# A fused two-layer forward and backward kernel: gradient-job operands stored feature-major and turned when they are loaded, normalised rows turned by SyncE

## The chip, the cores and the metric

The kernel runs on one core of one Trainium2 chip. The metric is the device time of one execution in microseconds (us). The engines are named as in the profile: PE is TensorE (PEld its weight loads), DVE VectorE, ACT ScalarE, POOL GpSimd, SP SyncE. SP and POOL also issue DMAs; in the profile's DMA tables SP's queue is q1 and POOL's is q0. All large data are bf16.

## The reference

Four residual layers are run forward, `x = x + A(norm(x))`, `x = x + B(norm(x))`, and both once more with the same weights, and then the gradients of all inputs are taken against `grad_out`. There are 2048 rows of 448 features; the hidden width of B is 1792.

```python
def _A_ref(q, k, v, shift_k, ssm_k, ssm_D):
    ...                                   # k_shift: causal 4-tap filter of k
    kv = k_shift * v
    ...                                   # y: long convolution of kv with ssm_k, by FFT
    y = y + kv * ssm_D[None, None, :]
    return q * y
def _B_ref(x, w1, w2):
    h = jnp.einsum("bsd,df->bsf", x, w1)
    h = _silu(h)
    return jnp.einsum("bsf,fd->bsd", h, w2)
x = A_q
x = x + _A_ref(_layernorm(x, axis=-1), A_k, A_v, A_shift_k, A_ssm_k, A_ssm_D)
x = x + _B_ref(_layernorm(x, axis=-1), B_w1, B_w2)
x = x + _A_ref(_layernorm(x, axis=-1), A_k, A_v, A_shift_k, A_ssm_k, A_ssm_D)
x = x + _B_ref(_layernorm(x, axis=-1), B_w1, B_w2)
```

The outputs are x and the gradients of q, k, v, shift_k, ssm_k, ssm_D, w1 and w2. `y` does not depend on x, so both A layers share it.

## The kernel before, in words

The work has three stages.

The **head** (class `Head`, up to about 95 us) computes `y` by matrix products that form an FFT.

The **flow** (class `Flow`, about 95 to 480 us) handles 16 tiles of 128 rows. For each tile `j`, `Flow.tile` lists: normalise, gate with y, normalise (n1); turn n1 so that features lie on partitions (`turn`); the up product with w1 (`up`, lines 645 to 655); silu and its slope (`silu`); the down product with w2 (`down`, L689); the same again for layer 2 with n3; then the backward pass, whose up product with w2T is in `grad_up` and whose down product with w1T is in `back`. It yields, in feature-major form (128 features on partitions, 14 feature blocks, 128 rows): the activations of the two B layers (`a1`, `a2`, tile `aT`) and the two hidden gradients (`gh1`, `gh2`, tile `ghT`). Three operands per tile are turned by PE in `turn`: n1, n3 and G2 (four transposes at L627 into PSUM, then one copy to SBUF by ACT or DVE at L92 or L94). The incoming gradient `g` is turned by two DMA transposes on SP (L757, L758).

The **tail** (class `Tail`, about 455 us to the end) has the backward FFT and the weight gradients. The weight gradient of w2 needs `a` with rows on partitions, and that of w1 needs `gh` with rows on partitions. So in the flow `store_turned` turns each of the four tensors of a tile with one DMA transpose from SBUF to SBUF (tile `turned`, L679) and stores the result row-major in DRAM (`A_d`, `GH_d`, L680). The tail's `jobs` then takes 7 jobs of 256 features per weight. A job loads two pieces of 1 MB (16 row tiles of 128 rows by 256 features, tile `jb`, L1072), one for each layer: group 0 is layer 2 (`A_d[1]` against `grad_out`, or `GH_d[1]` against n3), group 1 is layer 1 (`A_d[0]` against G2, or `GH_d[0]` against n1). It runs 64 products (L1124), 16 for each of two 128-feature halves and each group. In this text load (p, g) is that of job p and group g. `jb` has three buffers; every second job's load of group 0 for w1 goes to a fourth, in the place of `Minv`. The rows of n1 and n3 come back from DRAM as `nmov` (L1055). The last tile's activations are not read from DRAM by the first two w2 jobs: they take them from the `turned` tile itself (`lastA`).

The order is not written by hand. Each operation is listed with its costs per engine, its dependencies and a priority, and a planner (`Sched.plan`) simulates the engines: whenever an engine is free it takes, among the operations that are ready and have buffers, the one with the lowest priority number. A DMA's time in this simulation comes from `RATE` (bytes per us) and one shared time `dma_free`. The operations are emitted in the planned order; at run time each engine and each queue executes its list strictly in order and waits on semaphores. A tile's priorities are spaced by `T_ = 20`; layer 2 starts at `c = b + T_`, the first layer's gradient at `d = c + T_`. `BUFS` gives the number of buffers of each tag. `k.load` chains the job loads (`behind`), so that they are issued in the order in which they are listed.

Of the kernel before, what the change touches and what calls it, by code (L numbers as in the profile page):

```python
# [13 lines left out]
BF16 = mybir.dt.bfloat16  # L14
# [6 lines left out]
P = 128  # L21
S = 2048
D = 448
F = 1792
J = 16
NT = 16
DC = 112
ND = 4
# [104 lines left out]
class Sched:  # L133
# [4 lines left out]
    STEP = 20  # L138
    RATE = {"plain": 300e3, "turn": 160e3}

# [98 lines left out]
    def plan(self):  # L239
# [3 lines left out]
        events = [0.0]  # L243
        dma_free = 0.0
        for o in self.all:
# [26 lines left out]
        t = 0.0  # L272
        total = sum(1 for o in self.all if o.cost)
        while len(order) < total:
            moved = True
            while moved:
                moved = False
                for e, q in queue.items():
# [10 lines left out]
                    o = best  # L289
# [38 lines left out]
            t = events[0]  # L328
# [250 lines left out]

T_ = 20.0  # L580
EARLY = 2
ROWS = (0, 128, 256, 320)
TURNED = ((1, 0), (1, 1), (3, 0))


class Flow:
# [31 lines left out]

    def turn(self, src, pr, tag, after=()):
        nc, k, s = self.nc, self.k, self.s  # L620
        pt = s.vb("ps", "d", [P, ND, P], BF16, "ps_t")
        nT = self.small(tag, (P, ND, P))
        nT.name = "nT"

        def mm(e):
            for b, lo in enumerate(ROWS):
                nc.tensor.transpose(pt[:, b, :], src[:, lo:lo + P], k.ident[:])  # L627
# [47 lines left out]

    def store_turned(self, src, dst, j, pr):
        nc, s = self.nc, self.s
        an = self.small("turned", (P, NF, P))
        self.k.last_turn_out = s.op({"SP": 2.2}, lambda e: nc.sync.dma_start_transpose(out=an[:], in_=src[:].rearrange("p a s -> p (a s)")), r=[src], w=[an], prio=pr, dma=("turn", 458e3))  # L679
        s.op({"SP": 0.4}, lambda e: nc.sync.dma_start(out=dst[:, j, :], in_=an[:].rearrange("p a f -> p (a f)")), r=[an], w=[self.k.st_[(id(dst), j)]], prio=pr + 3, dma=("plain", 458e3))  # L680
        return an

# [41 lines left out]
    def tile(self, j):  # L724
        nc, s, k = self.nc, self.s, self.k
        b = T_ * j
# [11 lines left out]
        s.op({"POOL": 0.6}, lambda e: nc.gpsimd.dma_start(out=_pm(k.N_d[0][:])[:, j, :], in_=n1[:]), r=[n1], w=[k.st_[("n", 0, j)]], prio=b + 10, dma=("plain", 115e3))  # L738
        a1, s1 = self.silu(self.turn(n1, b - 3, "nT1"), 0, b, (j, 0) in TURNED)
        self.store_turned(a1, k.A_d[0], j, b + 4)  # L740
        po = self.down(a1, k.w2, "ps_o", b + 8.6)
# [10 lines left out]
        k.lastA_op = k.last_turn_out  # L752
        g = self.small("g")
# [6 lines left out]
        k.lastG = self.last_up  # L760
        self.store_turned(gh2, k.GH_d[1], j, c + 15)
        po2 = self.down(a2, k.w2, "ps_o", c + 14.2)
# [35 lines left out]
class Tail:  # L798
# [242 lines left out]
    def jobs(self, which, pr):  # L1041
        nc, s, k = self.nc, self.s, self.k
        if which == "w2":
            k.load = []
            gm = s.vb("res", "W1", [P, NT, D], BF16, "gmov")
            gs = [gm.sub() for _ in range(4)]
            gl = [lambda i=i: s.op({"SP": 0.4}, lambda e: nc.sync.dma_start(out=gm[:, 4 * i:4 * i + 4, :], in_=_pm(k.grad_out[0])[:, 4 * i:4 * i + 4, :]), w=[gs[i]], prio=pr - 30, dma=("plain", 458e3), behind=[k.lastA_op]) for i in range(4)]
            groups = [(k.A_d[1], [gs[t // 4] for t in range(NT)], lambda t: gm[:, t, :]), (k.A_d[0], k.G2v, lambda t: k.G2[:, t, :])]
        else:
            nm = [s.vb("PF", ("A1", "B1v")[i], [P, NT, D], BF16, "nmov") for i in range(2)]  # L1050
            nh = [[v.sub() for _ in range(2)] for v in nm]
            for i in (1, 0):
                for h in range(2):
                    hs = slice(8 * h, 8 * h + 8)
                    s.op({"SP": 0.4}, lambda e, i=i, hs=hs: nc.sync.dma_start(out=nm[i][:, hs, :], in_=_pm(k.N_d[i][:])[:, hs, :]),  # L1055
                         r=[k.st_[("n", i, j)] for j in range(8 * h, 8 * h + 8)], w=[nh[i][h]], after=self.done[i], prio=pr - 30 if i else pr + 0.5, dma=("plain", 917e3))
            groups = [(k.GH_d[1], [nh[1][t // 8] for t in range(NT)], lambda t: nm[1][:, t, :]), (k.GH_d[0], [nh[0][t // 8] for t in range(NT)], lambda t: nm[0][:, t, :])]
        out7 = k.outs[7].rearrange("(c p) f -> p c f", p=DC)
# [8 lines left out]
        def bring(p, gi, lo, hi, at=None):  # L1067
            b, part, spare = fetch(p, gi, which == "w1" and (2 * p + gi) % 4 == 0)
            src = groups[gi][0]
            v = b.sub()  # L1070
            part[lo:hi] = [v] * (hi - lo)
            k.load = [s.op({"SP": 0.4}, lambda e: nc.sync.dma_start(out=b[:, lo:hi, :], in_=src[:, lo:hi, 256 * p:256 * p + 256]),  # L1072
                 r=[k.st_[(id(src), j)] for j in range(lo, hi)], w=[v], prio=pr + 12.5 * p + gi if at is None else at, dma=("plain", 65e3 * (hi - lo)), behind=k.load, after=self.done[0] if spare else ())]

# [80 lines left out]
def kernel(  # L1155
# [22 lines left out]
    nc = tc.nc  # L1178
    k = K()
# [32 lines left out]
    with tc.manual_schedule(engines={E.PE, E.Activation, E.DVE, E.Pool, E.SP}):  # L1212
# [5 lines left out]
    "res": dict(W1=1, W2=1, G2=1, Y=1),  # L1218
    "J": dict(jb=3, oo=2),
    "S": dict(KK=1, A1K=1, A1v=1, pq=3, skb=1, skc=1),  # L1220
    "E": dict(x0=3, w2T=1, st=2, mv=6, ve=6, n0=5, t1=1, x1=3, n1=5, nT1=1),
    "PM": dict(w2Tr=1, w1T=1, nT3=1, nTg=2, nTG=1, s1=4, T=4, turned=3, x2=1, n2=3, x3=3, n3=3, s2=2, g=3, ghp=2, ob=2,
               u=3, cp=6, junk=1, cc=6, tt=1, G3=2, gy2=3, G1=1, gy=1, gq=2),
# [104 lines left out]
```

## Time and profile before

| | us |
|---|---|
| median of 3 runs | 720.97 (719.65 to 722.09) |
| profiled execution | 722.94 |
| its span, first to last instruction | 721.2 |
| PE busy in it | 695.1 (96%) |
| DVE busy | 516.7 (72%) |
| ACT busy | 419.8 (58%) |
| L627 transposes of n (128) and G (64), PE busy | 12.5 and 6.2 |

| DMA | count, KB each | us to landing |
|---|---|---|
| jb<-GH_d, SP | 14, 1024 | median 7.2 |
| jb<-A_d, SP | 12, 1024 | median 7.4 |
| turned<-aT and turned<-ghT, SP, transposes | 32 each | median 5.5 |
| A_d<-turned, SP | 32, 448 | median 3.9 |
| GH_d<-turned, SP | 32, 448 | median 4.2 |

(The profile's table counts by tensor name, so the 32 of each pair are the two layers' 16 tiles.) A row of the profile's timeline reads: start in us, length in us, engine, line, operation, output tile <- input tiles, shapes, count; the part in brackets is idle time of that engine before it and what ended it. PE's matrix products are pipelined: a product's length contains its drain, and the next one starts before it ends, so the pace is read from start to start. In the rows of 20 us the numbers are the busy time of PE, PEld, DVE, ACT and POOL with instruction counts, then the granted clock, the DMA engines' mean busy share and GB/s. The share of DMA can exceed 1, because a packet's time counts in the stretch in which it starts.

### The profile page before, as it was taken

What the parts mean: (1) busy time and instruction counts of PE and PEld (TensorE: products, weight loads), DVE (VectorE), ACT (ScalarE), POOL (GpSimd) and SP (SyncE); (2) the same over time, 40 slices, a digit from 0 to 9 for tenths busy, and PEclk for the clock granted to TensorE, in tenths of its full rate; (3) what the DMA queues carried; (4) which work ended last, traced back from release to release, by engine and by line L of the source; (5) the groups of instructions that cost most, each with busy time, mean ns of one, the idle gap of its engine ahead of it and who ended that gap; (6) DMA issues with size and microseconds to landing.
All of it is one profiled execution on the core that took longest, in us unless ns stands there. A gap on an engine that the chain in (4) does not pass through costs nothing. (4 is left out here: it accounts for less than half of the span.)

```text
span 721.2 us, 18320 instructions
## 1 busy us (share of the span) xinstructions
PE 695.1 (96%) x7664; PEld 484.8 (67%) x7664; DVE 516.7 (72%) x1215; ACT 419.8 (58%) x518; POOL 158.9 (22%) x266
## 2 busy tenths in 40 slices
PE   6999879999999999999999999999999999999997
PEld 5887657777777777777777776655576766555553
DVE  4989775669988889888988867671479857959100
ACT  4899876586667765776667755521676555111311
POOL 1244153112321233222321211003123203100000
PEclk9999998999999999999999999999999999999999
DMA  9989988899889898888878798979759949996751
GB/s 323 275 236 291 344 143 179 183 217 210 190 187 190 213 202 179 190 208 226 167 181 188 205 213 200 305 217 280 214 181 370 319 139 329 354 292 191 193 130 27
DMA packets 230720, 160.08 MB, mean 222 GB/s; under 512 B 145326, under 2 KB 207966, under 8 KB 230252
## 3 DMA queue, kind: packets, MB, share of 16 engines
q1 hardware_dynamic: 216862, 117.85, 66.6%
q0 software_dynamic: 13008, 40.24, 17.3%
q8 instruction: 60, 0.98, 0.6%
q10 hardware_dynamic: 766, 0.80, 0.3%
q14 instruction: 24, 0.20, 0.1%
HBM read 65.36 MB, written 54.60 MB: 166 GB/s over the span
## 5 line engine op out<-in xcount | busy, mean ns | idle before, releaser
L1124 PEld LDWEIGHTS <-jb 128*128 128x128 bf16 x892 | 85.7, 98 | 77.8 <-DMA jb<-GH_d 1.2
L645 PE MATMUL ps_h<-nT,w1sb 128*128 128x128 bf16 x1344 | 88.0, 222 | 5.7 <-DVE nT L94 4.9
L689 PE MATMUL ps_n<-w1T,ghT 128*128 128x448 bf16 x448 | 90.0, 352 | 1.4 <-ACT u L788 0.9
L689 PE MATMUL ps_o<-w2sb,aT 128*128 128x448 bf16 x448 | 90.1, 353 | 0.0
L645 PEld LDWEIGHTS <-w1sb 128*128 128x128 bf16 x1344 | 79.4, 99 | 14.5 <-DVE nT L94 4.8
L1124 PE MATMUL ps_d<-nmov,jb 128*128 128x448 bf16 x448 | 87.9, 353 | 0.8 <-DMA jb<-GH_d 0.8
L645 PE MATMUL ps_g<-nT,w2T 128*128 128x128 bf16 x1344 | 85.8, 219 | 0.7 <-ACT nT L92 0.7
L645 PEld LDWEIGHTS <-w2T 128*128 128x128 bf16 x1344 | 77.3, 98 | 7.4 <-issue 0.8
L701 ACT CAST ghp<-ps_g 128x896 bf16<-128x896 f32 x64 | 57.9, 907 | 39.0 <-PE ps_g L654 22.5
L673 ACT ACTIVATE aT<-ps_h 128x896 bf16<-128x896 f32 x64 | 56.9, 916 | 26.3 <-PE ps_h L654 19.7
L689 PEld LDWEIGHTS <-ghT 128*128 128x128 bf16 x448 | 42.6, 98 | 37.3 <-issue 1.8
L689 PEld LDWEIGHTS <-aT 128*128 128x128 bf16 x448 | 42.6, 98 | 35.1
L713 DVE SCALAR_TENSOR_TENSOR junk<-u,n 128x448 bf16<-128x448 bf16 x64 | 39.9, 623 | 32.5 <-ACT u L788 31.8
L673 ACT ACTIVATE dT<-ps_h 128x896 bf16<-128x896 f32 x64 | 57.1, 917 | 8.8 <-PE ps_h L645 5.3
L610 POOL TENSOR_TENSOR rstd<-ve,mhalf 128x1 f32<-128x1 f32 x64 | 45.5, 711 | 55.0 <-DVE ve L607 52.9
L1124 PE MATMUL ps_d<-G,jb 128*128 128x448 bf16 x224 | 45.5, 352 | 0.0
L1124 PE MATMUL ps_d<-gmov,jb 128*128 128x448 bf16 x220 | 45.0, 352 | 0.0
L673 ACT ACT_TABLE_LOAD x34 | 43.6, 1283 | 0.6
L92 ACT CAST dob<-ps_d 128x448 bf16<-128x448 f32 x14 | 7.5, 533 | 59.8 <-PE ps_d L1124 59.8
L702 DVE TENSOR_TENSOR ghT<-ghp,dT 128x896 bf16<-128x896 bf16 x64 | 38.5, 622 | 4.8 <-ACT ghp L701 4.8
L788 ACT ACTIVATE u<-ps_n,rstd 128x448 bf16<-128x448 f32 x32 | 20.4, 637 | 36.7 <-PE ps_n L689 36.7
L605 DVE BATCH_NORM_STATS2 st<-x 128x6 f32<-128x448 bf16 x64 | 39.9, 624 | 1.2
(174 smaller groups left out, 1258.4 us busy)
## 6 DMA issues: line engine op xcount, KB each, us to landing
A_d<-turned SPq DMA_DIRECT2D x32, 448.0 KB, 3.9
GH_d<-turned SPq DMA_DIRECT2D x32, 448.0 KB, 4.2
jb<-GH_d SPq DMA_DIRECT2D x14, 1024.0 KB, 7.2
jb<-A_d SPq DMA_DIRECT2D x12, 1024.0 KB, 7.4
KK<-KK POOLq DMA_DIRECT2D x14, 256.0 KB, 5.4
spec_K<-KK POOLq DMA_DIRECT2D x7, 512.0 KB, 6.5
spec_KV<-X POOLq DMA_DIRECT2D x7, 512.0 KB, 12.3
N_d<-n POOLq DMA_DIRECT2D x32, 112.0 KB, 3.6
```

What stands on the lines that cost most here:

```text
L92: nc.scalar.copy(out, in_)
L605: nc.vector.bn_stats(out=st[:], in_=x[:])
L610: s.op({"POOL": 1.0}, lambda e: nc.gpsimd.tensor_tensor(out=rs[:], in0=ve[:], in1=self.k.mhalf[:, 0:1], op=ALU.pow), r=[ve], w=[rs], prio=pr)
L645: nc.tensor.matmul(ps[:, i, :], lhsT=at(b, ft), rhs=nT[:, b, :], **f)
L673: prev = [s.op({"ACT": 0.93}, lambda e, i=i, fun=fun, out=out: nc.scalar.activation(out[:, 7 * i:7 * i + 7, :], h[i][:], fun), r=[h[i]], w ...
L689: nc.tensor.matmul(po[:, :D], lhsT=a[:, ft, :], rhs=wt[:, ft * D:(ft + 1) * D], start=(ft == 0), stop=(ft == NF - 1))
L701: s.op({"ACT": 0.93}, lambda e, i=i, t=t: nc.scalar.copy(t[:], G[i][:]), r=[G[i]], w=[t], prio=pr)
L702: s.op({"DVE": 0.57}, lambda e, i=i, t=t: nc.vector.tensor_tensor(out=gh[:, 7 * i:7 * i + 7, :], in0=t[:], in1=d[:, 7 * i:7 * i + 7, :], o ...
L713: nc.vector.scalar_tensor_tensor(out=junk[:], in0=u[:], scalar=1.0, in1=n[:], op0=ALU.mult, op1=ALU.mult, accum_out=cp[:, 1:2])
L788: s.op({"ACT": 0.85}, lambda e: nc.scalar.activation(u[:], pn[:, :D], ACT.Identity, scale=r[:], accum_out=cp[:, 0:1]), r=[pn, r], w=[u, cp ...
L1124: nc.tensor.matmul(ps[:, :D], lhsT=rows(t, gi, u), rhs=at(t), start=(first and t == ts[0]), stop=(last and t == ts[-1]))
```

## The change

The tensors of layer 2's activations (A1) and of both hidden gradients (GH0, GH1) are stored in DRAM as they lie in SBUF, feature-major (`[F, S]`), with a plain DMA in pieces of 128 rows (256 bytes). The tail's job loads of these three are DMA transposes from DRAM to SBUF. Layer 1's activations (A0) keep the old path. In the flow, n1, n3 and G2 are turned by a pair of DMA transposes on SP, except 12 listed in `ON_PE` (first index the tile, second 0 for n1, 1 for n3, 2 for G2), which PE still turns. `SKEW` adds 5 to the priorities of layer 2 and another 5 to those of the first layer's gradient. `lastA` becomes a small transpose of its own (4 feature blocks). `turned` has 2 buffers instead of 3, `nT3` and `nTG` 2 instead of 1. In the planner SP's and POOL's DMAs no longer share one `dma_free`, and there are rates for the new kinds.

```diff
-    RATE = {"plain": 300e3, "turn": 160e3}
+    RATE = {"plain": 300e3, "turn": 160e3, "load": 215e3, "rows": 180e3}
...
-                        dma_free = max(dma_free, o.end) + nbytes / self.RATE[kind]
-                        o.end = dma_free + 1.8
+                        dma_free[e] = max(dma_free[e], o.end) + nbytes / self.RATE[kind]
+                        o.end = dma_free[e] + 1.8
...
+SKEW = (5.0, 5.0)
+RAW = ("A1", "GH0", "GH1")
+ON_PE = ((0, 0), (0, 1), (0, 2), (1, 0), (1, 1), (1, 2), (2, 0), (13, 2), (14, 1), (14, 2), (15, 1), (15, 2))
...
-    def turn(self, src, pr, tag, after=()):
+    def turn(self, src, pr, tag, on_pe, after=()):
+        if not on_pe:
+            nT = self.small(tag, (P, ND, P))
+            nT.name = "nT"
+            s.op({"SP": 1.2}, lambda e: nc.sync.dma_start_transpose(out=nT[:, 0:3, :], in_=src[:, 0:384]), r=[src], w=[nT], prio=pr - EARLY, dma=("turn", 98e3))
+            s.op({"SP": 1.2}, lambda e: nc.sync.dma_start_transpose(out=nT[:, 3, :], in_=src[:, 320:448]), r=[src], w=[nT], prio=pr - EARLY, dma=("turn", 33e3))
+            return nT
...
+    def store(self, src, nm, j, pr):
+        nc, s, k = self.nc, self.s, self.k
+        dst = k.rows_d[nm]
+        if nm not in RAW:
+            self.store_turned(src, nm, j, pr)
+            return
+        at = dst.rearrange("(a p) s -> p a s", p=P)[:, :, P * j:P * j + P]
+        s.op({"SP": 0.45}, lambda e: nc.sync.dma_start(out=at, in_=src[:]), r=[src], w=[k.st_[(nm, j)]], prio=pr, dma=("rows", 458e3))
...
-        c = b + T_
-        a2, s2 = self.silu(self.turn(n3, c + 2.7, "nT3"), 1, c + 5.6, (j, 1) not in TURNED)
+        c = b + T_ + SKEW[0]
+        a2, s2 = self.silu(self.turn(n3, c + 2.7, "nT3", (j, 1) in ON_PE), 1, c + 5.6, (j, 1) not in TURNED)
...
-        k.lastA = self.store_turned(a2, k.A_d[1], j, c + 10)
+        if j == NT - 1:
+            k.lastA = s.vb("J", "lastA", [P, 4, P], BF16, "lastA")
+            k.lastA_op = s.op({"SP": 1.2}, lambda e: nc.sync.dma_start_transpose(out=k.lastA[:], in_=a2[:, 0:4, :].rearrange("p a s -> p (a s)")), r=[a2], w=[k.lastA], prio=c + 10, dma=("turn", 131e3))
+        self.store(a2, "A1", j, c + 10)
...
-        d = c + T_
-        gh1 = self.grad_up(self.turn(G2, d + 14, "nTG"), s1, d + 16.9)
-        self.store_turned(gh1, k.GH_d[0], j, d + 20)
+        d = c + T_ + SKEW[1]
+        gh1 = self.grad_up(self.turn(G2, d + 14, "nTG", (j, 2) in ON_PE), s1, d + 16.9)
+        self.store(gh1, "GH0", j, d + 20)
...
+            if nm in RAW:
+                cost, kind, get = 0.3 * n, "load", lambda e: nc.sync.dma_start_transpose(out=b[:, lo:hi, :], in_=src[fs, P * lo:P * hi])
+            else:
+                cost, kind, get = 0.4, "plain", lambda e: nc.sync.dma_start(out=b[:, lo:hi, :], in_=src[:, lo:hi, fs])
...
-    k.A_d = [dram.tile([P, NT, F], BF16, name=f"A_d{i}") for i in range(2)]
-    k.GH_d = [dram.tile([P, NT, F], BF16, name=f"GH_d{i}") for i in range(2)]
+    k.rows_d = {nm: dram.tile([F, S] if nm in RAW else [P, NT, F], BF16, name=f"{nm}_d") for nm in ("A0", "A1", "GH0", "GH1")}
```

More of the change, by code (lines that the diff above doesn't have):

```diff
@@ L243, in plan @@
         events = [0.0]
-        dma_free = 0.0
+        dma_free = defaultdict(float)
         for o in self.all:
@@ L760, in tile @@
         k.lastG = self.last_up
-        self.store_turned(gh2, k.GH_d[1], j, c + 15)
+        self.store(gh2, "GH1", j, c + 15)
         po2 = self.down(a2, k.w2, "ps_o", c + 14.2)
@@ L1056, in jobs @@
                          r=[k.st_[("n", i, j)] for j in range(8 * h, 8 * h + 8)], w=[nh[i][h]], after=self.done[i], prio=pr - 30 if i else pr + 0.5, dma=("plain", 917e3))
-            groups = [(k.GH_d[1], [nh[1][t // 8] for t in range(NT)], lambda t: nm[1][:, t, :]), (k.GH_d[0], [nh[0][t // 8] for t in range(NT)], lambda t: nm[0][:, t, :])]
+            groups = [("GH1", [nh[1][t // 8] for t in range(NT)], lambda t: nm[1][:, t, :]), ("GH0", [nh[0][t // 8] for t in range(NT)], lambda t: nm[0][:, t, :])]
         out7 = k.outs[7].rearrange("(c p) f -> p c f", p=DC)
@@ L1068, in bring @@
             b, part, spare = fetch(p, gi, which == "w1" and (2 * p + gi) % 4 == 0)
-            src = groups[gi][0]
+            nm = groups[gi][0]
+            src, n, fs = k.rows_d[nm], hi - lo, slice(256 * p, 256 * p + 256)
+            if nm in RAW:
+                cost, kind, get = 0.3 * n, "load", lambda e: nc.sync.dma_start_transpose(out=b[:, lo:hi, :], in_=src[fs, P * lo:P * hi])
+            else:
+                cost, kind, get = 0.4, "plain", lambda e: nc.sync.dma_start(out=b[:, lo:hi, :], in_=src[:, lo:hi, fs])
             v = b.sub()
             part[lo:hi] = [v] * (hi - lo)
-            k.load = [s.op({"SP": 0.4}, lambda e: nc.sync.dma_start(out=b[:, lo:hi, :], in_=src[:, lo:hi, 256 * p:256 * p + 256]),
-                 r=[k.st_[(id(src), j)] for j in range(lo, hi)], w=[v], prio=pr + 12.5 * p + gi if at is None else at, dma=("plain", 65e3 * (hi - lo)), behind=k.load, after=self.done[0] if spare else ())]
+            k.load = [s.op({"SP": cost}, get,
+                 r=[k.st_[(nm, j)] for j in range(lo, hi)], w=[v], prio=pr + 12.5 * p + gi if at is None else at, dma=(kind, 65e3 * n), behind=k.load, after=self.done[0] if spare else ())]
         if which == "w2":
```

21 lines of the change are left out of this document (10 added, 11 removed).

## The prediction

> **What bounds the kernel now.** I read the profile's page first, then the stretches of 20 us, then TensorE's timeline over one tile, then the chain of waits, and last the landing times of the DMAs that resemble the new ones. The page:
>
> ```profile
> PE 695.1 (96%) x7664; PEld 484.8 (67%) x7664; DVE 516.7 (72%) x1215; ACT 419.8 (58%) x518; POOL 158.9 (22%) x266
> PE   6999879999999999999999999999999999999997
> DMA  9989988899889898888878798979759949996751
> ```
>
> TensorE (PE) is busy 96% of the span, so most of what is taken off it ends up in the time, as long as nothing else becomes late. DMA is the second row to watch. The stretches, with PE busy first and the DMA share and GB/s last:
>
> ```profile
> 280.00:300.00 20.00, 20.00 (x269) 15.15 (x267) 17.25 (x52) 14.62 (x20) 4.98 (x8) 1.00 0.89 200
> ...
> 600.00:620.00 20.00, 19.89 (x205) 12.89 (x204) 14.49 (x26) 9.22 (x11) 5.69 (x10) 1.00 1.01 336
> 620.00:640.00 20.00, 19.19 (x162) 9.92 (x161) 17.13 (x30) 1.07 (x2) 2.90 (x5) 1.00 1.11 343
> ...
> 680.00:700.00 20.00, 20.00 (x116) 10.75 (x115) 0.00 (x0) 3.67 (x7) 0.00 (x0) 1.00 0.73 184
> ```
>
> In the tile flow (about 120 to 440 us) PE is full and DVE, next, has 2.75 of 20 us free. From 600 to 640 the DMA engines are full as well. One tile on PE, matmul rows only:
>
> ```profile
> 287.92 0.39 PE L627 MATMUL ps_t<-ident,n 128*128 128x128 bf16 x4
> 288.14 2.81 PE L689 MATMUL ps_n<-w1T,ghT 128*128 128x448 bf16 x14
> ...
> 297.56 0.39 PE L627 MATMUL ps_t<-ident,G 128*128 128x128 bf16 x4
> ...
> 302.21 0.39 PE L627 MATMUL ps_t<-ident,n 128*128 128x128 bf16 x4
> 302.43 1.34 PE L645 MATMUL ps_g<-nT,w2T 128*128 128x128 bf16 x21
> ...
> 310.98 0.39 PE L627 MATMUL ps_t<-ident,n 128*128 128x128 bf16 x4
> ```
>
> The pattern comes round after 310.98 - 287.92 = 23.06 us with no idle mark: PE alone sets the pace of a tile. It holds three turns. The 0.39 us is how long four pipelined transposes take to drain; what a turn delays is the step to the next start, 0.22 us for each turn of normalised rows (288.14 - 287.92) and 0.32 us for that of G2 (the next matmul, L654, starts at 297.88).
>
> Late in the kernel the chain of waits holds one long DMA piece, and PE's timeline shows the idle time at its end:
>
> ```profile
> 620.55 13.93 DMA jb<-GH_d
> 634.48 0.05 issue
> 634.52 4.71 PE ps_d L1124 x24
> ```
> ```profile
> 634.52 4.71 PE L1124 MATMUL ps_d<-nmov,jb 128*128 128x448 bf16 x24 [0.81 <-DMA jb<-GH_d]
> ```
>
> The second w1 load already comes 0.81 us late, in the stretch where DMA is full. A slower load there has no cover.
>
> **The change part by part.**
> *Turns off PE.* 48 turns, 12 kept by ON_PE, leave 36: 25 of normalised rows and 11 of G2 (tiles 2 to 12). That is 25 x 0.22 + 11 x 0.32 = 9.0 us off PE, all in or beside the full stretch: **-9.0**. The ACT or DVE copies behind them (587 and 421 ns) go too; both engines wait there anyway, so they count zero.
>
> *Turns on SP.* Each is two DMA_TRANSPOSE, like the present pair nT<-g: issue 1.68 and 1.23 us, landing 2.3 to 5.2 us, median 3.2. A turn so takes about 1.7 + 2.5 to 3.4, some 5 us, against 0.22 and a copy before. Now SP's queue is in order: behind a turn that waits for n1, n3 or G2 stand the stores, the gradient's turn and A0's turn; and an up matmul waits for it. SKEW moves layer 2 back by 5 us and the first layer's gradient by 10 in priority, about the added latency, and PE is saturated, so that other up and down products fill in. I count zero; without that cover each late turn costs PE up to 5.2 - 3.2 = 2 us beyond the median. SP's issue time per tile is now 4 x (1.75 + 1.1) + 2.9 = 14.3 us; afterwards 1.75 + 1.1 + 3 x 0.5 to 1.1 + 2.9 + 3 x 2.9 = 16 to 18 of 22.3. It fits, without much room.
>
> *Raw stores.* 48 stores lose their turn into `turned` and go out in 256-byte pieces, 1792 of them. No row has such a store. In the packet records of the trace a 256-byte packet of a transpose has a median of 18 ns, an 896-byte packet of a plain DMA 41. So a store takes 1792 x 18 / 16 = 2.0 us of the 16 engines, or 4.6 at most; a turned store takes 2.0 to 2.9 (mean packet 26 ns) plus 1.2. I take 2.0 to 2.5, by the row with the same size, and the flow's DMA gets lighter: zero. The Trainium skill, in "DMA: Bandwidth & Descriptors", Specifications, says that pieces under 512 B fall short of line rate because the engine reads, modifies and writes. No run here shows such a store; by that rule the upper end holds, which is the third rival's mechanism.
>
> *Job loads turned.* 21 loads of 1 MB (7 of A1, 14 of the gradients) are now transposes from DRAM. The nearest rows are w1T (802 KB, the same kind):
>
> ```profile
> L1277 SPq DMA_TRANSPOSE w1T<-in_B_w_dram x2: 4602/5877/7152, 87.2 to 101.2; - x2
> ...
> DMA to landing us min/median/max: 7.2/8.5/9.7
> ```
>
> The first of them landed 3.8 us after the transpose ahead of it, so 3.8 x 1024/784 = 5.0 us per load; jb loads now move at about 290 GB/s, 3.6 us. Bounds: 4096 packets of 256 B at 18 ns make 4.6, at the mean of 26 ns 6.7. I take 5.0: **+1.4 each**. The records also show a transpose's first 500 packets at 60 to 95 ns where it follows a large plain DMA, a stall of 1.5 to 2 us. The 7 A1 loads are issued 5 to 20 us apart beside filler work, and count zero. The w1 jobs are different. Loads (0,0) and (1,0) went through from 614 to 620.6; now about 614 to 625.4 with one stall. Then nmov, about 5 us as before, then a stall and load (0,1): its data end near 637 instead of 632, and it lands near 639 instead of 634.5. The product that started at 634.52 waits: **+4.5** (bounds 0, if the loads come no slower, and 10, at 6.7 us each). Next in line is (1,1), 5 us behind; the 6 us of products of (0,1) hide it. The Trainium skill ("Advanced Engine Details and Errata", X-Bar Transpose) says that transposes are as fast as ordinary DMAs here; by it this term would be zero and the time that of the first rival. The trace is against it: 18 ns for 256 B, 28 for 512 B.
>
> After that: 2 loads per job of 12.5 us on PE, 10 us plus a stall of about 1.5 plus 0.9 for the out store: 12.4, just within. Zero.
>
> *Order, start and drain.* Start and drain of the flow idle PE for 7.6 us (80 to 120) and 2.4 (440 to 480). The turns there stay on PE. Running layer 2 later may fill the start or lengthen the drain: 0, bounds -2 and +3. The smaller lastA turn (4 blocks instead of 14) only frees DMA.
>
> **Sum.** -9.0 + 4.5 = -4.5. The profiled execution took 722.94 us (span 721.2 and 1.7 around it), 2 above the median of 720.97; it becomes 718.4, and the median **716.5**.
>
> **Rivals.**
> *The loads stay hidden* (the late load is issued early enough, or transposes keep up): only the turns count, 720.97 - 9.0 = 712, down to 709 if the start fills as well. For it: PE has no other wait on jb. Against: the 0.81 us.
> *The last stage becomes DMA-bound* (the other side). From 609.5 to about 701.5, where the last load is used, the queue must move 14 loads, 4.7 us of nmov, 6 of out stores and 7 stalls of 1.5: 14 L + 21. At L = 5.0 that is 91 of 92 us; above it each 0.1 us per load costs 1.4 us, and at 5.7 the whole gain is gone. At the mean packet, L = 6.7, it is 115: +23 - 9 = 14, so 735.
> *The flow becomes DMA-bound by the raw stores.* Per tile, from the packet records: A0 4.1 (turn 2.9, store 1.2), four turns of 512 packets 3.3, POOL's six DMAs 2.3, and three raw stores; at 37 ns per piece these fill 22.3 us, and at 41 ns it is 23.5: 1.2 us late in each of 12 to 13 tiles, +15, or 731 with the other terms. Turns land late first, and PE shows idle time before L645. For it: DMA share 0.89 now; against: 256 B in 18 ns.
> That layout and turns could fail to take effect isn't seen: RAW names the tensors, and the stores and loads follow it.
>
> **How the numbers follow.** Forecast 0.45 (712.5 to 720), loads hidden 0.22, last stage bound 0.20 (720 to 735), flow bound 0.13 (719 to 731). This kernel's measurement tells about 0.3% from no change: 718.8 and 723.1. Faster: 0.45 x 0.92 + 0.22 + 0.13 x 0.1 = 0.65; same: 0.45 x 0.08 + 0.20 x 0.3 + 0.13 x 0.25 = 0.13; the rest slower, 0.22. Range 708.5 to 729; it leaves out the worst half of the DMA-bound cases.
>
> **What would show it.** Right: the tile's pattern comes round after about 22.3 us, no idle mark from 130 to 430, L627 down to 48 transposes, jb<-GH0/GH1 landing in 8 to 10 us, and PE idle of some 5 us before the second pair of w1 loads. Wrong: idle before L645 behind nT in the flow; raw stores landing in over 6 us; idle before L1124 at every job from 650 on; or no idle at all there.

## The result and the profile after

| | before | after |
|---|---|---|
| median, us | 721.53 (719.65 to 722.13) | 745.12 (740.27 to 746.29) |
| ratio | | 1.0319, 95% interval 1.0268 to 1.0370 |
| profiled execution, us | 722.94 | 740.27 |
| its span, us | 721.2 | 738.5 |

The change makes the kernel 3.2% slower; 716.5 us was forecast. The profiled execution is the fastest of the four of the changed kernel (the others took 744.42 to 746.29), so its trace accounts for 17.3 of the 23.6 us between the medians. (Line numbers from here on are those of the kernel after: L654 is the up product, L707 the down products, L1149 the products of the gradient jobs, L1092 a turned job load.) The page of the profile after, with PE's totals, its busy tenths, its granted clock and the DMA engines in 40 slices of 18.5 us:

```profile
PE 686.2 (93%) x7502; PEld 474.0 (64%) x7520; DVE 515.4 (70%) x1203; ACT 406.0 (55%) x494; POOL 155.2 (21%) x266
...
PE   6998879999999999999999999999729997999997
...
PEclk9999999999999999999999999999959999999999
DMA  9999877565777766666677689586999899979971
```

PE is busy for 8.9 us less (695.1 before), and the DMA engines are visibly lighter in the flow (6 and 7 where they showed 8 and 9). But the 29th and 30th slice, 517 to 554 us, show PE at 7 and 2 tenths, and the clock at 5 in the second of them. The stretches of 20 us, columns as before (PE, PEld, DVE, ACT, POOL busy, granted clock, DMA share, GB/s):

```profile
520.00:540.00 20.00, 10.47 (x123) 7.66 (x122) 9.89 (x13) 9.65 (x10) 4.66 (x8) 0.84 1.27 120
540.00:560.00 20.00, 11.40 (x111) 8.74 (x112) 11.68 (x14) 4.86 (x6) 3.76 (x6) 0.65 1.01 251
600.00:620.00 20.00, 18.20 (x196) 9.85 (x194) 17.03 (x31) 4.00 (x5) 3.49 (x6) 1.00 1.07 308
620.00:640.00 20.00, 15.76 (x145) 7.54 (x145) 16.99 (x30) 1.06 (x2) 2.38 (x4) 0.91 1.21 237
```

From 520 to 540 the DMA share is the highest of these rows, 1.27, and the bytes moved are the fewest, 120 GB/s: the DMA engines are occupied, not productive. Before, PE was busy for 19.29 and 19.10 us in these two stretches.

One tile on PE, by the starts of the same down product of layer 1 in successive tiles:

```profile
259.97 2.81 PE L707 MATMUL ps_o<-w2sb,aT 128*128 128x448 bf16 x14
...
282.36 2.81 PE L707 MATMUL ps_o<-w2sb,aT 128*128 128x448 bf16 x14
...
304.74 2.81 PE L707 MATMUL ps_o<-w2sb,aT 128*128 128x448 bf16 x14
```

The pattern now comes round after 22.38 us instead of 23.06. PE's two long pauses in the tail, from its timeline (idle time and what ended it in the brackets):

```profile
547.22 0.29 PE L903 MATMUL ps_v<-Gsb,pq 128*128 128x128 bf16 x1 [16.62 <-DVE pq L897]
```
```profile
626.38 3.10 PE L1149 MATMUL ps_d<-gmov,jb 128*128 128x448 bf16 x8 [4.24 <-DMA jb<-A_d]
```

The first is not a job at all: it is the backward FFT, whose products wait for DVE's `pq`. One step back on the timelines of DVE, SP and POOL:

```profile
545.93 1.23 DVE L897 TENSOR_TENSOR pq<-xx_c,sp_c 128x2048 bf16<-128x2048 bf16 x1 [15.79 <-DMA sp_c<-spec_KV]
```
```profile
519.37 16.79 SPq L1092 DMA_TRANSPOSE jb<-A_d  x1
```
```profile
520.34 0.54 POOL L877 DMA_DIRECT2D sp_c<-spec_KV  x1 [1.49 <-DVE pq L897]
...
524.52 0.53 POOL L870 DMA_DIRECT2D Minvs<-c_minv  x1
...
528.42 0.54 POOL L877 DMA_DIRECT2D sp_c<-spec_KV  x1 [2.75 <-DVE pq L897]
529.55 0.72 POOL L877 DMA_DIRECT2D sp_c<-spec_K  x1 [0.60 <-DVE pq L897]
547.46 0.54 POOL L877 DMA_DIRECT2D sp_c<-spec_KV  x1 [17.18 <-DVE pq L897]
```

A turned load of A1 is issued on SP at 519.37. Its issue alone lasts 16.79 us, and it lands after 34.9. In the same time POOL's queue brings the spectra (`sp_c`, 256 KB each) and the 1 MB of `Minvs`. The seven of these that are issued from 520.34 to 529.55 need 25.5 to 28.3 us to land, and the spectrum that the FFT waits for is the first of them, issued at 520.34. By the packet records POOL's queue moved 3.68 MB and SP's 1.71 MB in those 34.9 us, together 154 GB/s. Before, a plain job load issued at 547.11 beside 2.98 MB of POOL's landed in 14.2 us, and the two queues together moved 374 GB/s. The landing times of all turned job loads, from the view of line 1092:

```profile
L1092 SPq DMA_TRANSPOSE jb<-GH_d x14: 4136/4896/10014, 623.5 to 710.1; - x14
L1092 SPq DMA_TRANSPOSE jb<-A_d x7: 4649/5521/16790, 433.0 to 607.9; - x7
...
DMA to landing us min/median/max: 6.3/8.3/34.9
```

The median is harmless; the longest of the 21 makes the difference. A second long one, at 607.92, heads the last stage in the chain of waits, where before load (0,1) of `GH_d` stood with 13.93 us:

```profile
607.92 18.41 DMA jb<-A_d
626.33 0.05 issue
626.38 3.10 PE ps_d L1149 x8
```

By stages (cut at the start of the first up product and at the end of the last `ps_n` product of the flow):

| us | head | flow | tail |
|---|---|---|---|
| before | 95.5 | 387.1 | 238.5 |
| after | 95.6 | 379.7 | 263.2 |

The flow gains 7.4 us; the tail loses 24.7. PE's pauses of over 0.3 us in the tail add up to 26.0 us against 3.0 before, so 23.0 of the 24.7 are pauses. The granted clock was 0.65 over the 10 us behind the pause that ended at 547.22 and 1.00 over the 10 us after that; it was 0.86 over the 10 us behind the one that ended at 626.38. This accounts for the rest in direction; its size was not separated. It is also not only the FFT that is held up: by the last inverse product (`ps_v`) 360 of the 448 w2 products were done before, 265 after, so the w2 jobs end at 642 instead of 621 us, and the w1 jobs begin 21 us later.

### The profile page after: what moved, and what is told of

It is laid out like the page before. It is cut to its first block, busy times and chain, and to the rows that moved or that the text cites. A ratio compares the mean times of both kernels' runs of the same rounds, so it can differ in the third digit from the quotient of the medians.

```text
span 738.5 us, 18086 instructions
## 1 busy us (share of the span) xinstructions
PE 686.2 (93%) x7502; PEld 474.0 (64%) x7520; DVE 515.4 (70%) x1203; ACT 406.0 (55%) x494; POOL 155.2 (21%) x266
## 5 line engine op out<-in xcount | busy, mean ns | idle before, releaser
L1149 PEld LDWEIGHTS <-jb 128*128 128x128 bf16 x892 | 86.0, 98 | 83.2 <-DMA jb<-A_d 4.7
L654 PE MATMUL ps_h<-nT,w1sb 128*128 128x128 bf16 x1344 | 87.2, 221 | 6.3 <-DVE nT L94 5.4
L707 PE MATMUL ps_o<-w2sb,aT 128*128 128x448 bf16 x448 | 90.0, 352 | 0.0
L707 PE MATMUL ps_n<-w1T,ghT 128*128 128x448 bf16 x448 | 90.0, 352 | 0.0
L1149 PE MATMUL ps_d<-nmov,jb 128*128 128x448 bf16 x448 | 87.4, 353 | 0.0
L654 PEld LDWEIGHTS <-w1sb 128*128 128x128 bf16 x1344 | 78.1, 99 | 13.3 <-DVE nT L94 4.6
L654 PE MATMUL ps_g<-nT,w2T 128*128 128x128 bf16 x1344 | 85.6, 219 | 0.0
L654 PEld LDWEIGHTS <-w2T 128*128 128x128 bf16 x1344 | 77.1, 98 | 6.3
L613 POOL TENSOR_TENSOR rstd<-ve,mhalf 128x1 f32<-128x1 f32 x64 | 42.7, 667 | 121.2 <-DVE ve L610 120.9
L707 PEld LDWEIGHTS <-ghT 128*128 128x128 bf16 x448 | 42.7, 98 | 35.8
L707 PEld LDWEIGHTS <-aT 128*128 128x128 bf16 x448 | 42.5, 98 | 35.1
L1149 PE MATMUL ps_d<-gmov,jb 128*128 128x448 bf16 x220 | 47.0, 360 | 4.2 <-DMA jb<-A_d 4.2
L1149 PE MATMUL ps_d<-G,jb 128*128 128x448 bf16 x224 | 46.3, 356 | 0.5 <-DVE nT L94 0.5
L903 PE MATMUL ps_v<-Gsb,pq 128*128 128x128 bf16 x224 | 28.7, 226 | 19.2 <-DVE pq L897 19.0
L897 DVE TENSOR_TENSOR pq<-xx_c,sp_c 128x2048 bf16<-128x2048 bf16 x28 | 33.1, 1222 | 18.6 <-DMA sp_c<-spec_KV 15.8
```

The costliest lines, as they stand in the source:

```text
L613: s.op({"POOL": 1.0}, lambda e: nc.gpsimd.tensor_tensor(out=rs[:], in0=ve[:], in1=self.k.mhalf[:, 0:1], op=ALU.pow), r=[ve], w=[rs], prio=pr)
L654: nc.tensor.matmul(ps[:, i, :], lhsT=at(b, ft), rhs=nT[:, b, :], **f)
L707: nc.tensor.matmul(po[:, :D], lhsT=a[:, ft, :], rhs=wt[:, ft * D:(ft + 1) * D], start=(ft == 0), stop=(ft == NF - 1))
L897: s.op({"DVE": 1.15}, lambda e, i=i, pq=pq: nc.vector.tensor_tensor(out=pq[:], in0=xx(), in1=sp[i][:].unsqueeze(1).to_broadcast([P, 2, 102 ...
L903: nc.tensor.matmul(pv[:, m, :], lhsT=pq[:, 0, m * P:(m + 1) * P], rhs=k.Gsb[:, G_IAC, :], start=True, stop=False)
L1149: nc.tensor.matmul(ps[:, :D], lhsT=rows(t, gi, u), rhs=at(t), start=(first and t == ts[0]), stop=(last and t == ts[-1]))
```

## The experiments

Two theories stood at the start. **Mixing** (theory 1 in the expectations): a turned load in flight beside transfers of another queue makes both slow, so POOL's spectra come late. **Layout** (theory 2): the turned loads are slow as such, or the raw stores are. A third, **order** (theory 3), came from the change's small print: the planner no longer shares one `dma_free`, so it now places job loads where it believes POOL's queue to be independent.

| kernel | us | ratio to before, 95% | head / flow / tail of the profiled execution, us |
|---|---|---|---|
| before | 721.53 | | 95.5 / 387.1 / 238.5 |
| after | 745.12 | 1.0319 (1.0268 to 1.0370) | 95.6 / 379.7 / 263.2 |
| A1 stored turned again | 745.43 | 1.0330 (1.0291 to 1.0369) | 99.2 / 397.8 / 246.3 |
| spectra on SP | 728.59 | 1.0106 (1.0069 to 1.0143) | 99.3 / 379.5 / 247.8 |
| all 48 turns on PE, no skew | 747.52 | 1.0347 (1.0305 to 1.0390) | 98.9 / 387.5 / 260.9 |
| one planner clock | 731.48 | 1.0155 (1.0134 to 1.0175) | 95.4 / 380.7 / 255.4 |
| spectra and four stores on SP | 722.80 | 1.0033 (1.0013 to 1.0054) | 97.5 / 379.6 / 243.9 |
| before, with spectra on SP | 721.29 | 1.0000 (0.9986 to 1.0015) | 95.3 / 387.2 / 238.2 |
| one clock, spectra on SP | 728.52 | 1.0107 (1.0092 to 1.0122) | 95.3 / 380.3 / 251.1 |
| one clock, spectra and stores on SP ("repaired") | 721.75 | 1.0005 (0.9988 to 1.0022) | 95.6 / 378.9 / 244.0 |
| repaired, no skew | 751.64 | 1.0419 (1.0396 to 1.0442) | 95.4 / 408.5 / 247.3 |
| repaired, all turns on PE, no skew | 729.97 | 1.0119 (1.0098 to 1.0139) | 95.1 / 387.5 / 245.6 |

The head needs care. With the planner's separate clocks it took 95.6 us in one profile and 97.5 to 99.3 in the other four; with one clock 95.1 to 95.6. The changed kernel and the one with the spectra on SP run PE's products of the head in the same order and yet differ there by 3.7 us, so what sets it is not shown. What an edit does to the tail is therefore read from the tail, and not from the total alone.

### The transfers by themselves

A kernel that holds only DMAs, in phases with a barrier between them. The job is four loads of 1 MB, turned or plain; the company is 12 transfers of 256 KB.

```
phase(turned, None, None)            phase(plain, None, None)
phase(None, spec, nc.gpsimd)
phase(turned, spec, nc.gpsimd)       phase(plain, spec, nc.gpsimd)
phase(turned, spec, nc.sync, True)   phase(plain, spec, nc.sync, True)   # in between, on SP
phase(turned, stored, nc.gpsimd)     phase(plain, stored, nc.gpsimd)     # stores instead of loads
```

> Leaves the whole computation out and writes zeros; it only moves data, in nine phases kept apart by barriers. A phase is 4 job loads of 1 MB on SP's queue (turned: 256 x 2048 feature-major, or plain: row-major in 512-byte pieces), 12 transfers of 256 KB between DRAM and SBUF in 2 KB rows (loads as sp_c, or stores), or both at once, the 12 on POOL's queue or in between on SP's own. Theory 1, two queues: a DMA transpose that runs beside steady traffic of another queue slows both far beyond a sharing of bandwidth. It expects 4 turned loads alone in 20 to 23 us, 4 plain ones in 15 to 17, the 12 loads alone in 9 to 11, plain with POOL's in 21 to 26, turned with POOL's in over 42, and turned with the same 12 loads between them on SP's queue in 30 to 38. Theory 2, load size: turned loads are just slower, whatever runs beside them; turned with POOL's takes about the sum, 29 to 34, and no more on one queue than on two.

The phases in this order (length, DVE, POOL, clock, DMA share, GB/s; the last two are those with the stores):

```profile
54.00:74.80 20.80, 0.00 (x0) 0.00 (x0) 1.00 0.99 202
74.90:92.10 17.20, 0.00 (x0) 0.00 (x0) 1.00 0.98 244
92.20:104.10 11.90, 0.00 (x0) 6.41 (x12) 1.00 0.77 264
104.20:143.50 39.30, 0.00 (x0) 6.49 (x12) 1.00 1.14 187
143.60:168.80 25.20, 0.00 (x0) 6.48 (x12) 1.00 1.00 291
168.90:200.50 31.60, 0.00 (x0) 0.00 (x0) 1.00 1.02 233
200.60:225.90 25.30, 0.00 (x0) 0.00 (x0) 1.00 1.00 290
226.00:262.80 36.80, 0.00 (x0) 6.40 (x12) 1.00 1.10 200
262.90:286.00 23.10, 0.00 (x0) 6.40 (x12) 1.00 1.00 318
```

Alone, four turned loads take 20.8 us against 17.2, 21% more. Beside POOL's 12 loads, plain ones take 25.2 us, less than the 29.1 of the two one after the other; turned ones take 39.3, more than the 32.7 of the two one after the other. Through SP's own queue the same bytes take 31.6, a little under that sum. Beside POOL's stores turned loads take 36.8 and plain ones 23.1. So a turned load gains next to nothing from company, and POOL's queue as the company costs 6.6 us on top of the sum. The figure of theory 1, over 42 us, was not reached; its order of the phases was. This speaks for mixing, and against "slow as such" as the main cause.

### A1 stored row-major again

```diff
-RAW = ("A1", "GH0", "GH1")
+RAW = ("GH0", "GH1")
```

> The changed kernel, but layer 2's activations take the old way again (turned to rows in the flow, plain job loads); the gradients stay feature-major and the turns stay on SP. Theories 1 and 2: no turned load is left in the stretch of the backward FFT, so PE's stall of 16.6 us behind sp_c goes with the clock dip that follows, and the 14.7 us issue of the load at 608 too: 745 - 18 to 25 = 720 to 727; PE idle under 3 us between 500 and 600. Theory 3, order: the stall comes from the planner, which now counts the two queues apart and places sp_c and Minvs beside job loads; the kernel stays at 738 to 746.

745.43 us: as slow as the change, but elsewhere. The time is the one that theory 3 gave (738 to 746) and not the 720 to 727 of the other two, but theory 3's reason, the pause beside the spectra, is not in it. The FFT's pause is gone: PE waits 3.0 us for `pq` in the tail instead of 19.0, and the last `ps_v` ends only 3 us after that of the change although the flow ended 22 us later. The planner's clocks are still separate and the spectra still on POOL, so with plain A1 loads these two alone do not make the pause. The flow took 397.8 us instead of 379.7. PE's waits between 110 and 480, and SP's timeline in one tile:

```profile
PE ps_h L654 <- DMA nT<-n: 14.1, 7, 3.8
```
```profile
271.81 2.01 SPq L698 DMA_TRANSPOSE turned<-aT  x1
278.32 0.34 SPq L699 DMA_DIRECT2D A_d<-turned  x1
279.56 1.18 SPq L627 DMA_TRANSPOSE nT<-G  x1
```

The turns of n1 and n3 come late, which they did not in the change (0.7 us in all between 130 and 440). With one more turned store per tile SP has a second turn and a second store that waits for it: here the store stands 4.5 us at the head of the queue (273.82 to 278.32) and the turn of G2 behind it. That this wait and not the added issue time is the larger part wasn't isolated. The raw layout is at least what gives SP the room for the row turns.

### The spectra through SP

The 28 `sp_c` loads and `Minvs` are issued by SP instead of POOL, so that no POOL load lies beside the A1 loads.

```diff
-            s.op({"POOL": 0.6}, lambda e, ...: nc.gpsimd.dma_start(out=sp[i][:], ...
+            s.op({"SP": 0.45}, lambda e, ...: nc.sync.dma_start(out=sp[i][:], ...
```

> The changed kernel with the 28 loads of sp_c and the load of Minvs in the tail issued by SP instead of POOL, so that they stand in one queue with the turned job loads. Theory 1: the turned loads in the FFT stretch land in 7 to 11 us each again (one took 34.9), PE's stall of 16.6 us behind sp_c goes, and some 2 us stalls where the queue changes kind take its place: 722 to 733. Theory 2: as many bytes and as slow loads, so the stall stays: 738 to 748. Theory 3 makes no forecast of a removal either, as the planner still places them side by side: 735 to 748.

728.59 us, 16.5 below the change, as theory 1 had it (722 to 733); the tail is 15.4 us shorter. The two stretches that collapsed:

```profile
520.00:540.00 20.00, 18.79 (x206) 13.56 (x208) 18.49 (x24) 13.11 (x15) 0.73 (x1) 1.00 1.15 270
540.00:560.00 20.00, 19.78 (x193) 13.62 (x195) 16.09 (x21) 11.03 (x12) 0.72 (x1) 1.00 1.13 328
```

PE's waits for `pq` (L903) fall from 19.0 to 1.5 us, and the A1 loads after 500 us land in 10.8 to 12.9. The tail is still 9.3 us longer than before. PE waits 5.2 us for `gK`, a copy by ACT of the backward FFT, which was not followed further, and 4.2 us in the next place where the queues meet: the first three `GH_d` loads, beside POOL's output stores, land in 14.3, 12.4 and 14.5 us.

The same edit in the kernel before, where the job loads are plain, is the control:

> A control: the kernel before the change, with sp_c and Minvs on SP. It has no turned load in the tail. Theory 1: nothing to gain from one queue, 719 to 724, the same as before within 0.4%. If spec_sp gained only because SP issues faster than POOL or because the plan differs, this one gains too: under 716.

721.29 us, ratio 1.0000 (0.9986 to 1.0015). The queue of the spectra is worth nothing by itself; it is worth 15 to 16 us only where the loads beside them are turned.

### All turns back on PE

```diff
-ON_PE = ((0, 0), (0, 1), (0, 2), (1, 0), ...
+ON_PE = tuple((j, i) for j in range(16) for i in range(3))
-SKEW = (5.0, 5.0)
+SKEW = (0.0, 0.0)
```

> The changed kernel with all 48 turns on PE again and no skew: only the layout and the turned job loads are left of the change. If the turns are worth 9.0 us on PE and all the loss lies in the turned loads, the tile's pattern comes round after 23.05 us again, PE busy rises by 9, and the time is 745 + 9 = 750 to 757. If the loss came from the skew or from the turns on SP, it is near the kernel before: 718 to 726.

747.52 us, under the 750 to 757 expected: without any turn on SP the loss is all there, and the flow is at 387.5 us, where it was before the change (387.1). So the 7.4 us of the flow belong to the turns with their skew, and the loss to the layout with its turned loads and to what the planner does with them. PE again waits for `pq`, 14.8 us.

### One planner clock again

```diff
-                        dma_free[e] = max(dma_free[e], o.end) + nbytes / self.RATE[kind]
-                        o.end = dma_free[e] + 1.8
+                        dma_free[0] = max(dma_free[0], o.end) + nbytes / self.RATE[kind]
+                        o.end = dma_free[0] + 1.8
```

> The changed kernel, but the planner counts SP's and POOL's DMAs on one clock again, as before the change; layout, turns and skew stay. Theory 3, order: the two clocks are what puts the sp_c loads beside a turned load and what sets the head 3.5 us later; with one clock the FFT stretch has no stall over 3 us and the time is 722 to 732. Theory 1, two queues: the loads stay turned and POOL's traffic stays, so some turned load of the tail still meets it; the place of the stall may move, but the tail from the last ps_n product to the end stays at 255 us or more (before: 238.5), and the time is 736 to 750.

731.48 us, inside theory 3's 722 to 732. The spectra stay on POOL and the loads stay turned, yet 13.6 us come back by the medians, 7.8 of them seen in the tail of the profiled executions: the plan puts A1 loads at 511.4 and 543.2, none between them, and they meet 0.23 and 1.14 MB of POOL's instead of 3.68. The meeting is not gone: the next load, at 562.2, lands after 21.9 us, and 3.8 of PE's 4.4 us of waiting for `pq` come then. The tail is 255.4 us long, as theory 1 had it (255 or more), though its 736 to 750 for the whole was missed. The rest of the waiting sits at the first w1 loads, which meet 1.39 and 1.61 MB of POOL's stores:

```profile
PE ps_d L1149 <- DMA jb<-GH_d: 11.6, 2, 8.9
```

Only a part of this is the loads' slowness (12.0 and 13.4 us to landing). Load (0,0) goes into the buffer of `Minv`, and the kernel lets it start when the last `ps_gK` product has read that. It is issued at 615.2, after the w2 products, which should cover it, had ended at 614.1. Before, it was issued at 609.5 and they ended at 621.0.

### Both, and the stores too

> spec_sp with the planner's single DMA clock. If the head's 3.5 us come from the plan with two clocks, the first up product starts near 95.5 us instead of 99 and the time is 722 to 726; if the head's difference is run to run, it equals spec_sp, 726 to 733. Theory 1 sees no new stall in either.

One clock and the spectra on SP: 728.52 us, no better than the spectra alone (728.59), and not the 722 to 726 expected if the head came back, although it did (95.3 us). The two edits take away the same pause, and one wait of 14.3 us for `GH_d` beside POOL's stores remains: load (0,0) is issued at 609.1, when the w2 products have ended (608.2), and lands after 15.7 us. So the four output stores of the tail (`out_2`, `out_3`, `out_5`, `out_8`) go to SP as well, first with the planner's separate clocks:

```diff
-            s.op({"POOL": 0.6}, lambda e, ...: nc.gpsimd.dma_start(out=out3[:, sl, :], in_=gv[:]), ...
+            s.op({"SP": 0.45}, lambda e, ...: nc.sync.dma_start(out=out3[:, sl, :], in_=gv[:]), ...
```

> The changed kernel with sp_c and Minvs on SP as in spec_sp, and the tail's large stores (gradients of k, v, ssm_k and w2) issued by SP as well, so that POOL's queue carries next to nothing in the tail. Theory 1: the 9.3 us that spec_sp's tail still has over the kernel before come from turned gradient loads beside POOL's stores (they land in 12 to 14.5 us at 610 to 640, 6.2 to 8 where nothing runs beside them); now they land in 7 to 10 and the tail shrinks from 248 to 240 to 244: 719 to 725. Rival: SP's queue is in order, and stores that wait for ACT and DVE now hold up the loads behind them; then PE waits before the w2 and w1 products in many places, 728 to 742.

722.80 us; the first four `GH_d` loads land in 7.5 to 10.4 us. Then with one clock, the "repaired" kernel:

> The changed kernel with both repairs: the tail's sp_c, Minvs and large stores on SP's queue (as in spec_outs_sp) and the planner's single DMA clock (as in shared_dma). If the two repairs add, the head starts the tiles at 95.4 us, the flow keeps its 7 to 8 us, and the tail is some 4 us longer than before for the first turned gradient loads: 715 to 719, a little under the kernel before (720.7). If the plan with one clock brings the w1 loads closer to the stores in SP's queue (shared_spec_sp waited 14.3 us for them in one place), 722 to 728.

721.75 us, equal to before: 1.0005 (0.9988 to 1.0022), 12 runs; neither the 715 to 719 nor the 722 to 728 of the expectation. Its waits for job loads, and SP's timeline at the w1 start:

```profile
PE ps_d L1149 <- DMA jb<-GH_d: 7.8, 3, 3.3
```
```profile
606.49 4.12 SPq L1092 DMA_TRANSPOSE jb<-GH_d  x1
610.70 0.99 SPq L986 DMA_DIRECT2D out_dram<-gK  x2
611.79 1.54 SPq L1175 DMA_DIRECT2D out_dram<-do  x1
613.42 1.66 SPq L1018 DMA_DIRECT2D out_dram<-gkp  x1
615.13 5.84 SPq L1092 DMA_TRANSPOSE jb<-GH_d  x1
```

By stages its profiled execution has 95.6, 378.9 and 244.0 us: 8.2 won in the flow, 5.5 lost in the tail against before, where the 7.8 us of waiting for the first w1 loads stand against 0.81. Most of these 7.8 us are not the price of slow loads. Load (0,0) is issued at 606.49, when the last `ps_gK` product frees its buffer, and lands in 6.1 us, against 10.5 before; but the w2 products end at 608.6 instead of 621.0, and PE waits 3.3 us. Behind it on SP stand four output stores, the last of which waits for DVE, so load (1,0) is issued only at 615.13, and PE waits 3.0 us. Load (0,1) costs the other 1.5. So this wait comes from the order of the plan and, as the rival in the expectation of "spectra and four stores on SP" had it, from the stores in SP's queue. Why this plan runs the w2 products earlier was not looked into.

### The skew and the turns in the repaired kernel

```diff
-SKEW = (5.0, 5.0)
+SKEW = (0.0, 0.0)
```

> one_queue_one_clock with SKEW = (0, 0): layer 2 and the first layer's gradient at their old priorities, turns still on SP. If the skew is what covers the turns' 5 us on SP, PE waits for nT in the flow by 0.3 to 1.5 us per tile and the flow is 5 to 20 us longer: 722 to 738. If PE's backlog covers them anyway, no difference over 3 us.

751.64 us, 29.9 more than repaired and beyond the 722 to 738 expected; the flow takes 408.5 instead of 378.9. PE's waits from 170 to 440, and ACT in one of these places:

```profile
PE ps_g L664 <- ACT aT L682: 20.9, 11, 1.9
```
```profile
205.47 0.92 ACT L682 ACTIVATE dT<-ps_h 128x896 bf16<-128x896 f32 x1 [0.37 <-PE ps_h L654]
206.40 1.28 ACT L682 ACT_TABLE_LOAD   x1
207.70 1.73 ACT L682 ACTIVATE aT<-ps_h 128x896 bf16<-128x896 f32 x2
```

PE does not wait for a turn: that of G2, issued at 204.28, had landed 2.3 us later. It waits in each of 11 tiles for ACT to clear a PSUM buffer, with a table load of 1.28 us in between, because this order runs three up products with no down product between them. These waits are 20.9 of the 29.6 us that the flow is longer; the rest was not separated. So the skew is needed, but the larger part of its effect is through the order of products that the planner writes, not through the lateness of a transfer.

```diff
-ON_PE = ((0, 0), (0, 1), (0, 2), (1, 0), ...
+ON_PE = tuple((j, i) for j in range(16) for i in range(3))
-SKEW = (5.0, 5.0)
+SKEW = (0.0, 0.0)
```

> one_queue_one_clock with all 48 turns on PE and no skew, so that only the turns' place differs. By the sum of the prediction 36 turns on PE cost 9.0 us (measured in the flow so far: 387.5 - 379.7 = 7.8): 7 to 10 us above one_queue_one_clock, 722 to 729. If the turns on SP cost elsewhere what they save on PE, the two are equal within 2 us.

729.97 us: with the loads repaired, the turns on SP, with the skew that goes with them, are worth 729.97 - 721.75 = 8.2 us.

### Which queue, how much, how large

A second kernel of DMAs alone, with the same four loads: company of 12 x 256 KB on ACT's queue, and on POOL's of 12 and 24 x 256 KB and of 6 x 1 MB.

```
phase(turned, spec, nc.scalar)     phase(plain, spec, nc.scalar)
phase(turned, spec, nc.gpsimd)
phase(None, twice, nc.gpsimd)      phase(turned, twice, nc.gpsimd)   phase(plain, twice, nc.gpsimd)
phase(None, big, nc.gpsimd)        phase(turned, big, nc.gpsimd)
```

> Leaves the whole computation out and writes zeros, as mb1 does; nine phases apart by barriers: 4 turned loads alone; turned, then plain job loads, with 12 loads of 256 KB on ACT's queue; turned with the 12 on POOL's queue; 24 loads on POOL's queue alone, with turned, with plain loads; 6 loads of 1 MB on POOL's queue alone and with turned loads. In mb1 turned alone took 20.9 us, the 12 alone 12.0, both 39.4 on two queues and 31.7 on one. If any second queue does it, turned with ACT's 12 takes 36 to 42; if only POOL's queue does, 29 to 33. If the loss lasts as long as the other traffic, turned with POOL's 24 takes 55 us or more, against 24 alone in 22 to 24 and 35 to 40 with plain loads; if it is a fixed cost of meeting, 50 to 52. The same with the 1 MB loads (6 MB alone 18 to 22): 55 or more against 42 to 48.

```profile
73.90:105.90 32.00, 0.00 (x0) 0.00 (x0) 1.00 1.14 229
106.00:130.70 24.70, 0.00 (x0) 0.00 (x0) 1.00 1.03 297
130.80:167.80 37.00, 0.00 (x0) 6.51 (x12) 1.00 1.10 198
167.90:193.70 25.80, 0.00 (x0) 13.03 (x24) 1.00 0.74 244
193.80:239.30 45.50, 0.00 (x0) 13.03 (x24) 1.00 1.09 231
239.40:273.80 34.40, 0.00 (x0) 13.05 (x24) 1.00 0.98 305
273.90:292.60 18.70, 0.00 (x0) 3.18 (x6) 1.00 0.89 336
292.70:336.80 44.10, 0.00 (x0) 3.23 (x6) 1.00 1.05 238
```

The turned loads alone took 19.9 us here; the plain loads alone (17.2) and the 12 transfers alone (11.9, on POOL's queue; those on ACT's were not run alone) are taken from the first kernel. With ACT's queue the turned loads take 32.0, the sum (19.9 + 11.9). With POOL's: 37.0 against 31.8, 45.5 against 45.7, 44.1 against 38.6. Plain loads stay under their sums (24.7 against 29.1; 34.4 against 43.0). So the sum is about the best that a turned load reached beside either queue, and POOL's cost up to a fifth more. Neither form of the loss that was expected, one that lasts as long as the company (55 us or more with 24 transfers) or a fixed one (50 to 52), shows in the 45.5 us. None of these phases is as slow as the 154 GB/s of the kernel. In that place SP's other loads and the FFT's own traffic lie in the same queues; why it is worse still stays open.

## Why the prediction was wrong

**The steps that held.** *Turns off PE, -9.0*: PE's busy time fell by 8.9 us, the flow by 7.4, the tile to 22.38 us (22.3 forecast), and the turns are worth 8.2 us in the repaired kernel. *The turns' lateness at zero*: 0.7 us of waiting from 130 to 440. Only the reason for SKEW was wrong, as its removal in the repaired kernel shows. *Raw stores at zero*: they land in a median of 4.0 and 4.2 us, against 3.9 and 4.2 before with a turn of 5.5 ahead of them; the DMA share from 130 to 440 went from 0.87 to 0.68. The third rival is out. The upper end, 41 ns a piece, which the prediction put beside the rule on pieces under 512 B in the Trainium skill ("DMA: Bandwidth & Descriptors", Specifications), is not what the packet records show: the 256-byte packets of SP's queue from 130 to 440, more than half of them these stores', have a median of 18 ns. In engine time a piecewise store is still the dearer one, by an estimate from these medians 1792 x 18 / 16 = 2.0 us against 128 x 140 / 16 = 1.1 us for a row-major one; the turn that it saves outweighs this. *A turned load at 5.0 us and the last stage just within*: 20.8 us for four alone, and from 640 us to the end PE pauses twice for 0.68 us, neither time for a load. The second rival is out: it forecast a slower kernel, but by another mechanism.

**The step that failed** is the sentence "The 7 A1 loads are issued 5 to 20 us apart beside filler work, and count zero". The work beside them on PE was looked at, the transfers beside them were not. One of the seven, issued into POOL's spectra, took 34.9 us and held the spectra up with it: PE stood for 16.6 us, the w2 products slipped by 95, and the last w2 load, among POOL's stores, cost 4.2 more. L = 5.0 was taken from w1T, a row that ran with no such company, and bounded by 6.7 from packet times. No bound of the sum allowed a load to depend on what POOL's queue does. Taking that away returns 16.5 us (spectra on SP), and the control, and the kernel with plain A1 loads, show that it needs the turned loads.

**The part that had no term** is the planner's clock. The change's text names it, the sum doesn't. With one clock and the same loads the kernel takes 13.6 us less, 7.8 of it in the tail, where the loads are placed elsewhere. The pause of 16.6 us needs both causes: turned loads that don't share, and a plan that takes the queues for independent and puts a load among the spectra. Removing the first returns 15.4 of the tail's 24.7 us, removing the second 7.8, and removing both 12.1, no more than the first alone.

**The term that was not met** is the start of w1, +4.5. In the change its place was taken by the late w2 load. Where the rest is repaired PE waits 7.8 us there, inside the bounds of 0 to 10, but this is luck: the prediction gave loads (0,0) and (1,0) no wait and had (0,1) late behind them, and the waits are 3.3 and 3.0 us for the first two, which are issued late for their products, and 1.5 us for (0,1). With the 8.2 of the turns the tail's loss of 5.5 leaves almost nothing: the repaired kernel's profiled execution is 2.7 us shorter in span than that of before, its median the same within 0.2%. The Trainium skill ("Advanced Engine Details and Errata", X-Bar Transpose) has transposes as fast as ordinary DMAs; the runs here have 20.8 against 17.2 us alone and 39.3 against 25.2 beside POOL's loads.

No kernel of this study is faster than the one before beyond the measurement.

## What to carry to other kernels

Before plain loads are replaced by DMA transposes, list what the other queues move in the same microseconds and add those times up instead of letting them overlap; a price taken from a transpose that ran without company is a lower bound. In the profile, a stretch with a DMA share above 1 and few GB/s is the sign, and the victim may be a transfer of another queue that feeds a different stage. When a planner's model of a resource is changed along with the code, the change of the plan is a term of its own: run the new code with the old model, and the other way round. And when a repair moves transfers into another queue, read again what now stands ahead of each load and how much work still covers it.

## What the runs showed of the hardware

- A DMA transpose beside another queue took about the sum of both times at best (32.0 and 45.5 us against sums of 31.8 and 45.7), and beside POOL's queue up to 20% more (39.3 against 32.7); plain loads took 13 to 20% less than the sum (25.2 against 29.1; 34.4 against 43.0).
- The issue of a 1 MB turned load on SP is not a fixed price: 4.1 to 5.2 us alone in the kernels of DMAs, 16.79 us beside POOL's loads, during which SP issues nothing else. Nor is that of a plain one: a median of 0.52 us for the gradient loads before, but 9.79 for the load at 621.16.
- Stores in 256-byte pieces from SBUF to DRAM (448 KB each) landed in a median of 4.0 to 4.2 us, much as the row-major stores before (3.9 and 4.2).
- After PE's pause of 16.6 us its granted clock was 0.65 over the next 10 us and 1.00 over the 10 after that, and the first FFT products took 314 ns instead of 219, so this pause cost more than its length.
